# First six blocks of a gated linear attention as three pairs with two tokens per partition, in an order written out as a list

## Chip, cores and metric

One NeuronCore of a Trainium2 chip (trn2) runs the kernel; seven are idle. The metric is the device time of one execution in microseconds. The profile is of one execution, taken by the hardware profiler; its time and its span (first to last instruction) are both given below. Engines are named PE (TensorE; PEld its weight loads), DVE (VectorE), ACT (ScalarE), POOL (GpSimd) and SP (SyncE, which here only issues DMAs).

## Reference

```python
def _attn_ref(q, k, v, alpha):            # each (4, 8, 768, 48) float32
    state = np.zeros((B, H, D, D))
    for t in range(S):
        state = alpha[:, :, t, :, None] * state + np.einsum('bhd,bhe->bhde', k[:, :, t], v[:, :, t])
        y[:, :, t] = np.einsum('bhd,bhde->bhe', q[:, :, t], state)

def _moe_ref(x, w_in, w_out, s, b):       # x is y as (3072, 384); w_in (384, 2048), w_out (2048, 384)
    r = np.maximum(x @ w_in, 0.0)
    return (s * (r * r) + b) @ w_out
```

A gated linear attention (4 sequences, 8 heads of 48 channels, 768 steps) is followed by a two-layer block with a squared relu on its 3072 x 384 output.

## The kernel before, in words

The 3072 tokens are 24 blocks of 128; six blocks are one sequence. In a block a partition holds one token. Each block goes through a chain of small steps, whose functions are named `st_...`:

- `load` (L192) brings alpha, q, k and v as `a_in`, `q_in`, `k_in`, `v_in`: 128 x 8 rows of 48 floats, 192 bytes each, from SP's queue. `NIN` = 5 buffers of each.
- `st_ln` (L299, ACT) takes the logarithm of alpha into `la`; `st_cum` (L304, PE) sums it along the block by a product with an upper triangle, into `ct_ps`, and the last row by four products with a column of ones; `st_exp_b` and `st_exp_i` (L319, L322, ACT) make the decay `b_s`, its inverse `binv` and the block's total `blast`.
- `st_qb`, `st_kb` (L332, L337, DVE) scale q and k into `qk`; `st_vcast` (L326, POOL) casts v into `vp`.
- `st_T` with `st_Tcopy` (L345, L372: eight PE transposes and a DVE copy) turns `qk` into `qkT` for the first `NPE` = 8 blocks; for the others `st_Tdma` (L354) does it by a DMA transpose.
- `st_KV` (L360, PE), `st_t1` (L380, DVE) and `st_snew` (L396, POOL) carry the state `s_st` on.
- `st_A` (L402, PE) forms the scores in `a_ps`, `st_mask` (L414, DVE) masks them into `am`, `st_y` (L433, PE) forms the output transposed in `py_ps` from scores and old state, `st_yevac` (L466, ACT) copies it to `xd`. From block `NAY` = 9 on, `st_Ay` puts the scores of a block and the output of the one before it together.

Then the second part, by groups of blocks (`GROUPS`): `mm1` (L484) makes units of 512 columns (six products of 256 columns, or twelve of 128 in a group of one block) into one of two banks `h_ps`; `relu` (L498, ACT) and `square` (L501, DVE) follow, the result goes into a ring `gt` of 12 blocks; `mm2` (L510) makes a block's output in four quads of four products of 384 columns, in one of two banks `o_ps`; `oevac` (L523, DVE) scales it and adds the bias row; `ostore` (L535) stores it. The weights come in eight pieces of 768 KB through four staging buffers `wst`, are cast to bf16 by ACT (`cast_w_in` L247, `cast_w_out` L260), and the column sums of w_out for the bias are made by DVE (`colsum_part` L267, `colsum_add` L273) and a product (`bias_mm` L285).

What sets the order: every step is handed to `Schedule.op` (L51) with a duration, a priority (the block's due time plus an offset of the table `P`), and what it reads and writes. `Schedule.run` (L68) plays these through, and `emit` (L118) writes the instructions in the order of the starts so found; the first loads stand in the order of the list `LOADS` (L41). Where PE would idle ahead of the first `mm2`, `fill` (L683) puts in products of zeros of 256 columns (45 in all). On the chip each engine takes its instructions in that order.

## Time and profile before

| | |
|---|---|
| three runs | 194.94 us median (193.78 to 196.74) |
| the profiled execution | 193.93 us |
| its span, mean granted PE clock | 192.0 us, 0.991 |
| busy: PE, PEld, DVE, ACT, POOL | 175.3, 126.7, 135.9, 109.5, 33.3 us |
| DMA | 124,218 packets, 34.44 MB; 117,536 packets under 512 B |
| loads of a, q, k, v | 24 each, 192 KB, 3.7 to 3.9 us from issue to landing |
| weight loads | 8, 768 KB, 7.0 and 8.4 us |
| DMA transposes | 16, 3.7 us |

How to read it: times are microseconds from the span's start. A row of a group has the line, the engine, output and inputs, the shapes, the count, then busy time and the mean duration in ns, then the engine's idle time ahead of it and what ended that. Products are pipelined, so their durations overlap; the pace is read from the starts. The chain of waits follows the work that ended last back from the end, at each step to what released it. A DMA share of 1 means that the 16 DMA engines' packets together fill the time.

### The profile page before, as it was taken

What the parts mean: (1) busy time and instruction counts of PE and PEld (TensorE: products, weight loads), DVE (VectorE), ACT (ScalarE), POOL (GpSimd) and SP (SyncE); (2) the same over time, 40 slices, a digit from 0 to 9 for tenths busy, and PEclk for the clock granted to TensorE, in tenths of its full rate; (3) what the DMA queues carried; (4) which work ended last, traced back from release to release, by engine and by line L of the source; (5) the groups of instructions that cost most, each with busy time, mean ns of one, the idle gap of its engine ahead of it and who ended that gap; (6) DMA issues with size and microseconds to landing.
All of it is one profiled execution on the core that took longest, in us unless ns stands there. A gap on an engine that the chain in (4) does not pass through costs nothing.

```text
span 192.0 us, 5369 instructions
## 1 busy us (share of the span) xinstructions
PE 175.3 (91%) x2153; PEld 126.7 (66%) x2153; DVE 135.9 (71%) x256; ACT 109.5 (57%) x225; POOL 33.3 (17%) x60
## 2 busy tenths in 40 slices
PE   1877688879999999999999999999999999999992
PEld 0555467657677767777777766776766876777761
DVE  4643299989799898877689868587777786554421
ACT  3254789984357847767475754763663763654300
POOL 8402022103120431201122313011131131000000
PEclk9996999999999999999999999999999999999999
DMA  6989979999999999999999998897998895011112
GB/s 122 203 219 317 312 161 245 353 223 205 196 232 193 219 140 213 197 214 188 196 160 209 145 236 188 171 207 169 208 197 195 164 180 144 3 43 41 40 45 82
DMA packets 124218, 34.44 MB, mean 179 GB/s; under 512 B 117536, under 2 KB 122656, under 8 KB 124192
## 3 DMA queue, kind: packets, MB, share of 16 engines
q1 hardware_dynamic: 124192, 34.09, 82.6%
q8 instruction: 17, 0.28, 0.6%
q14 instruction: 9, 0.07, 0.1%
HBM read 25.17 MB, written 4.72 MB: 156 GB/s over the span
## 4 chain that ended last, share of the span: by engine, by line
PE 66%; DMA 14%; DVE 8%; SPq 7%; ACT 2%; issue 1%
PE o_ps L515 29%; PE h_ps L490 25%; PE py_ps L444 5%; DMA wst<-in_moe_w_in_dram 4%; DMA q_in<-in_q_dram 4%; SPq L194 4%; DMA wst<-in_moe_w_out_dram 3%; PE a_ps L406 3%; SPq L240 3%; DMA qkT<-qk 3%; DVE am L415 2%; PE py_ps L364 2%; PE ct_ps L306 1%; DVE gt L506 1%; ACT r L499 1%
## 5 line engine op out<-in xcount | busy, mean ns | idle before, releaser
L490 PE MATMUL h_ps<-xd,w_in_bf 128*128 128x256 bf16 (+1 forms) x624 | 74.8, 264 | 0.8 <-ACT r L499 0.5
L499 ACT ACTIVATE r<-h_ps 128x512 bf16<-128x512 f32 x96 | 56.5, 601 | 32.3 <-PE h_ps L490 22.8
L515 PE MATMUL o_ps<-w_out_bf,gt 128*128 128x384 bf16 x384 | 72.8, 326 | 2.0 <-ACT w_out_bf L261 2.0
L490 PEld LDWEIGHTS <-w_in_bf 128*128 128x128 bf16 x624 | 54.7, 98 | 10.8 <-issue 1.2
L506 DVE TENSOR_TENSOR gt<-r 128x512 bf16<-128x512 bf16 x96 | 43.5, 465 | 21.7 <-ACT r L499 21.1
L515 PEld LDWEIGHTS <-gt 128*128 128x128 bf16 x384 | 36.0, 98 | 21.2 <-issue 2.3
L415 DVE TENSOR_TENSOR am<-a_ps,mask 128x1024 bf16<-128x1024 f32 x24 | 29.3, 1220 | 1.6 <-PE a_ps L406 1.4
L327 POOL CAST vp<-v_in 128x384 bf16<-128x384 f32 x24 | 13.3, 553 | 95.0 <-DMA v_in<-in_v_dram 84.7
L526 DVE SCALAR_TENSOR_TENSOR o_sb<-o_ps,s_col,bias_w 128x384 f32<-128x384 f32 x24 | 14.8, 616 | 10.0 <-PE o_ps L515 9.6
L300 ACT ACTIVATE la<-a_in 128x384 bf16<-128x384 f32 x24 | 12.5, 521 | 14.1 <-DMA a_in<-in_alpha_dram 13.9
L400 POOL TENSOR_TENSOR s_st<-t,blast 128x384 bf16<-128x384 bf16 x16 | 14.5, 909 | 30.8 <-DVE t L389 23.0
L468 ACT ACTIVATE xd<-py_ps 128x384 bf16<-128x384 f32 x24 | 11.8, 491 | 13.0 <-PE py_ps L444 12.8
L338 DVE TENSOR_TENSOR qk<-k_in,binv 128x384 bf16<-128x384 f32 x24 | 13.4, 558 | 6.7 <-ACT binv L323 5.5
L333 DVE TENSOR_TENSOR qk<-q_in,b_s 128x384 bf16<-128x384 f32 x24 | 13.5, 564 | 5.2 <-ACT b_s L320 4.1
L320 ACT ACTIVATE b_s<-ct_ps 128x384 f32<-128x384 f32 x24 | 11.7, 488 | 6.8 <-PE ct_ps L311 6.7
L389 DVE TENSOR_TENSOR t<-py_ps,s_st 64x192 bf16<-64x192 f32 x32 | 11.3, 353 | 3.9 <-PE py_ps L364 3.2
L306 PE MATMUL ct_ps<-la,U_bf 128*128 128x384 bf16 x24 | 8.0, 334 | 6.3 <-ACT la L300 6.3
L323 ACT ACTIVATE binv<-ct_ps 128x384 f32<-128x384 f32 x24 | 11.8, 490 | 0.0
L311 PEld LDWEIGHTS <-la 128*128 128x128 bf16 x96 | 6.0, 97 | 7.7 <-issue 5.6
L406 PE MATMUL a_ps<-qkT 64*128 64x128 bf16 x192 | 9.8, 222 | 1.0 <-DVE qkT L373 0.7
L406 PEld LDWEIGHTS <-qkT 64*128 64x128 bf16 x192 | 5.5, 96 | 7.3 <-issue 4.3
L444 PE MATMUL py_ps<-am,vp 128*32 128x128 bf16 x384 | 9.8, 224 | 0.5 <-DVE am L415 0.5
(42 smaller groups left out, 108.1 us busy)
## 6 DMA issues: line engine op xcount, KB each, us to landing
a_in<-in_alpha_dram SPq DMA_DIRECT2D x24, 192.0 KB, 3.9
q_in<-in_q_dram SPq DMA_DIRECT2D x24, 192.0 KB, 3.9
k_in<-in_k_dram SPq DMA_DIRECT2D x24, 192.0 KB, 3.9
v_in<-in_v_dram SPq DMA_DIRECT2D x24, 192.0 KB, 3.7
out_dram<-o_sb SPq DMA_DIRECT2D x24, 192.0 KB, 2.6
wst<-in_moe_w_in_dram SPq DMA_DIRECT2D x4, 768.0 KB, 8.4
wst<-in_moe_w_out_dram SPq DMA_DIRECT2D x4, 768.0 KB, 7.0
qkT<-qk SPq DMA_TRANSPOSE x16, 3.7
```

Source lines behind the costliest of these rows:

```text
L327: nc.gpsimd.tensor_copy(out=vp_sb[n % 4].rearrange("a p (x d) -> a p x d", d=D)[:, :, 0:3:2, :], in_=v_in[n % NIN].rearrange("a (p e) d -> ...
L333: nc.vector.tensor_tensor(out=qk_sb[n % 3][:, 0, :, 0:D], in0=q_in[n % NIN], in1=b_sb[n % 2], op=ALU.mult)
L338: nc.vector.tensor_tensor(out=qk_sb[n % 3][:, 1, :, 0:D], in0=k_in[n % NIN], in1=binv_sb[n % 2], op=ALU.mult,)
L400: nc.gpsimd.tensor_tensor(out=s_sb[n % 3], in0=t1_sb[n % 2], in1=bl, op=ALU.mult)
L406: nc.tensor.matmul(out=a_ps[:, e, p, :], lhsT=qkT[64 * e : 64 * e + 64, 1, p, :], rhs=qkT[64 * e : 64 * e + 64, 0, p, :], start=True, stop ...
L415: nc.vector.tensor_tensor(out=am_sb[n % 2].rearrange("a e p t -> a (e p) t"), in0=a_ps.rearrange("a e p t -> a (e p) t"), in1=mask.unsquee ...
L444: nc.tensor.matmul(out=y_ps[32 * (x % 4) : 32 * (x % 4) + 32, x // 4, :], lhsT=(st[:, p, c0 : c0 + 32] if e is None else vp[:, p, c0 + 48 ...
L490: nc.tensor.matmul(out=hp[:, i * n : (i + 1) * n], lhsT=w_in_bf[:, kk, 128 * j : 128 * (j + 1)], rhs=xd_sb[g % 3][:, kk, 0:n], start=(kk = ...
L499: nc.scalar.activation(out=r_sb[w % 2], in_=h_ps[w % 2], func=AF.Relu)
L506: nc.vector.tensor_tensor(out=gt_sb[:, js[0] : js[0] + len(js), c0 : c0 + n], in0=r, in1=r, op=ALU.mult)
L515: nc.tensor.matmul(out=op[:, 0:d_model], lhsT=gt_sb[:, j, c0 : c0 + C], rhs=w_out_bf[:, j, :], start=(j == 0), stop=(j == NJ - 1),)
L526: nc.vector.scalar_tensor_tensor(out=ots, in0=o_ps[(x // 4) % 2][:, 0:d_model], scalar=s_col, in1=bias_w, op0=ALU.mult, op1=ALU.add,)
```

## The change

The first six blocks (one sequence) become three pairs. In a pair a partition holds two neighbouring tokens, so that a load brings rows of two tokens (384 bytes), and partitions 0 to 63 are the first block, 64 to 127 the second. Each step of the pair has its own function (`ld2`, `ln2`, `cum2`, `blk2`, `eb2`, `ei2`, `el2`, `vc2`, `mul2`, `T2`, `Tc2`, `KV2`, `A2`, `mk2`, `y2`); sums, scores and outputs are made for both tokens and both halves. The sums of pair 1 stand in the banks `h_ps`, those of the others in `ct_ps` and `py_ps`; scores use `a_ps` and `o_ps`. All 18 later blocks are transposed by DMA (`T1`), and scores and output go together from block 7 on (`Ay`). All groups of the second part have two blocks. There are three pair buffers of each input (`NIN` = 6), the ring holds 8 blocks, and two of the w_out pieces are staged in parts of the ring that are not yet in use.

The planner is gone: `PROGRAM` lists every step in order, with the engine for those that can run on several. Casts of weights, casts of v, relus, squares, column sums and some products with the decay now stand on ACT, DVE or POOL by name: of 96 squares 73 on DVE, 15 on ACT, 8 on POOL; of 96 relus 78 on ACT, 18 on DVE. Products of zeros (`F`, 120 columns) stand at three places, 33, 19 and 16 of them, behind the cumulative sums of pairs 0 and 1; none stands ahead of the first sum.

In the list a name is followed by its arguments: `ld2.a.0` loads alpha of pair 0, `ld_i.3` the fourth quarter of w_in, `ci`/`co` cast a quarter of w_in/w_out, `cp`/`ca` are the column sums, `mm1.g.u.w` is unit u of group g into bank w, `re.g.u.w.i` and `sq.g.u.i` are its relu from bank w into buffer i and its square from there, then the engine, `mm2.n.j` is quad j of block n, `ye`, `oe`, `st` evict y, evict and store the output of a block.

```diff
-GROUPS = [2, 1, 1, 2, 2, 2, 2, 2, 2, 2, 2, 2, 2]
+NPAIR = 3
+GROUPS = [2, 2, 2, 2, 2, 2, 2, 2, 2, 2, 2, 2]
+NIN = 6
-RING = 12
+RING = 8
 NST = 4
+STAGE = {0: 0, 1: 1, 2: 2, 3: 3, 6: 0, 7: 1}
+STAGE_GT = {4: 2, 5: 3}
+CUM_IN_H = [1]
-class Schedule:
...
+PROGRAM = """
+ld2.a.0 c_act c_U2 c_la.1 c_la.0 ld2.a.1 c_zeros ld2.v.0 c_half c_qk.0 ld2.q.0 c_t1.0 c_qk.1 c_mask2
+ld2.k.1 ld2.k.0 c_s.0 ld2.q.1 ln2.0 c_s.1 ld2.q.2 c_t1.1 ld_i.3 cum2.0.0 c_ident ld2.v.1 ln2.1 cum2.0.1
+c_U c_ones blk2.0 c_vp.1 eb2.0.1 cum2.1.0 c_s.2 ei2.0.0 cum2.1.1 c_vp.0 blk2.1 ei2.0.1 vc2.0.1.POOL
+el2.0 vc2.0.0.DVE eb2.1.0 mul2.q.0.1.DVE ei2.1.0 eb2.1.1 el2.1 mul2.k.1.0.DVE ei2.1.1 eb2.0.0
+mul2.k.1.1.DVE mul2.q.0.0.DVE mul2.k.0.0.DVE F.33 T2.0.0 mul2.k.0.1.DVE mul2.q.1.1.POOL KV2.0 ld1.k.7
+Tc2.0.0.ACT ld_i.1 T2.0.1 t1.0 mul2.q.1.0.POOL ld_i.2 ld2.a.2 t1.1 ld1.k.6 Tc2.0.1.DVE ld_i.0 ld2.k.2
+sn.1.DVE F.19 A2.0.0 ld_o.0 A2.0.1 ci.3.POOL mk2.0.0 ld1.a.6 ld2.v.2 mk2.0.1 F.16 T2.1.0 vc2.1.1.ACT
+vc2.1.0.POOL T2.1.1 Tc2.1.0.ACT Tc2.1.1.DVE y2.0 A2.1.0 ye.0.DVE ye.1.ACT A2.1.1 mk2.1.0 KV2.1 ci.1.ACT
+mm1.0.6.0 t1.2 mm1.0.7.1 re.0.6.0.0.ACT ld_o.3 mk2.1.1 sn.2.POOL ld1.a.7 re.0.7.1.1.ACT mm1.0.3.0 ld_o.1
+ci.2.ACT mm1.0.2.1 t1.3 sq.0.6.0.DVE sn.3.POOL y2.1 re.0.3.0.0.DVE sq.0.7.1.ACT ln2.2 re.0.2.1.1.DVE
+mm1.0.5.0 ye.2.DVE sq.0.3.0.ACT mm1.0.4.1 ye.3.ACT sq.0.2.1.DVE cum2.2.1 re.0.5.0.0.ACT ci.0.POOL
+cum2.2.0 blk2.2 re.0.4.1.1.ACT sq.0.5.0.DVE mm1.1.5.0 eb2.2.0 sq.0.4.1.DVE mm1.1.4.1 ei2.2.0
+re.1.5.0.0.DVE ld_o.2 eb2.2.1 mul2.k.2.0.POOL re.1.4.1.1.DVE mm1.0.0.0 el2.2 ei2.2.1 mul2.q.2.1.DVE
+mm1.1.0.1 sq.1.4.1.POOL sq.1.5.0.ACT co.0.DVE re.0.0.0.0.ACT mul2.k.2.1.POOL re.1.0.1.1.ACT mm1.1.2.0
+mul2.q.2.0.DVE ln1.6 sq.1.0.1.DVE mm1.1.1.1 cp.0.POOL re.1.2.0.1.DVE T2.2.1 vc2.2.1.ACT T2.2.0
+sq.1.2.1.DVE vc2.2.0.ACT mm1.1.3.0 re.1.1.1.1.DVE sq.0.0.0.POOL Tc2.2.1.ACT KV2.2 Tc2.2.0.DVE mm1.1.7.1
+sq.1.1.1.ACT co.3.POOL t1.4 re.1.3.0.0.ACT A2.2.0 A2.2.1 ln1.7 mk2.2.0 mm1.0.1.0 re.1.7.1.1.ACT ld1.a.13
+sn.4.POOL ld1.q.6 sq.1.7.1.ACT mm1.1.6.1 mk2.2.1 ld1.q.8 cp.3.POOL re.0.1.0.1.ACT ld_bs co.1.DVE y2.2
+cp.1.POOL sq.0.1.1.DVE ye.5.ACT ye.4.DVE mm2.0.0 co.2.ACT ld1.v.8 re.1.6.1.1.DVE cum1.6 ld1.a.10
+mm1.2.5.0 sq.1.3.0.POOL cp.2.DVE ld1.q.7 mm1.2.0.1 ld1.a.8 ei1.6 ca.2.3.DVE ld1.v.6 ca.0.1.POOL mm2.0.1
+eb1.6 ld1.k.8 sq.1.6.1.ACT cum1.7 re.2.5.0.0.DVE ld1.a.9 mm2.0.2 ei1.7 ld1.v.9 bm mm1.2.2.0 ld1.a.11
+re.2.0.1.1.DVE eb1.7 vc1.8.POOL ld1.v.7 mm2.0.3 sq.2.5.0.ACT ca.0.2.DVE sq.2.0.1.ACT mm1.2.3.1 ln1.10
+re.2.2.0.0.DVE bmm re.2.3.1.1.ACT mul1.q.7.DVE sq.2.2.0.ACT sq.2.3.1.DVE mm1.2.1.0 ln1.8 mul1.k.6.DVE
+cum1.8 bc re.2.1.0.0.ACT mm1.2.7.1 vc1.6.POOL mul1.q.6.DVE eb1.8 mm1.2.4.0 oe.0 T1.6 sq.2.1.0.ACT KV1.6
+mm2.1.0 re.2.7.1.1.ACT re.2.4.0.0.DVE ln1.9 mm2.2.0 t1.6 st.0 sq.2.7.1.ACT mm2.2.1 mul1.q.8.DVE
+vc1.9.POOL ei1.8 mm1.2.6.1 mul1.k.7.DVE sq.2.4.0.ACT mul1.k.8.DVE cum1.9 T1.7 ln1.11 mm2.1.1
...
+    def ld2(x, m):
+        b, c = 2 * m // NCH, 2 * m % NCH
+        nc.sync.dma_start(
+            out=whole(ins[x], m).rearrange("a s e -> a (s e)").rearrange("a (h f) -> a h f", h=H),
+            in_=src[x][b, :, c * C : (c + 2) * C, :].rearrange("h (p s) d -> p h (s d)", s=2),
+        )
...
+    def stage(i):
+        if i in STAGE_GT:
+            return gt_sb[STAGE_GT[i]].bitcast(FP32)[:, 0:QW]
+        return wst[STAGE[i]]
...
+    def ci(i, eng="ACT"):
+        copy_on(
+            eng,
+            w_in_bf[:, :, QW // 3 * i : QW // 3 * (i + 1)],
+            stage(i).rearrange("a (k f) -> a k f", k=3),
+        )
...
+    def b_ps(m, s):
+        return (h_ps if m in CUM_IN_H else (ct_ps, py_ps))[s]
...
+    def cum2(m, s):
+        l = whole(la, m)
+        for i in range(2):
+            nc.tensor.matmul(
+                out=b_ps(m, s)[:, 0 : H * D],
+                lhsT=U2x if i > s else U2,
+                rhs=l[:, i, :, 0:D],
+                start=(i == 0),
+                stop=(i == 1),
+            )
...
+    def blk2(m):
+        l = whole(la, m).rearrange("a s h d -> a s (h d)")
+        for p in range(NP):
+            for i in range(2):
+                nc.tensor.matmul(
+                    out=b_ps(m, 0)[:, 384 + 2 * p : 386 + 2 * p],
+                    lhsT=l[:, i, 128 * p : 128 * p + 128],
+                    rhs=half,
+                    start=(i == 0),
+                    stop=(i == 1),
+                )
...
+    def T2(m, x):
+        f = whole(qk, m)[:, :, x].rearrange("a s h d -> a s (h d)")
+        t_ps = a_ps[:, x, :].bitcast(BF16).rearrange("a (s p t) -> a s p t", s=2, p=NP)
+        for s in range(2):
+            for p in range(NP):
+                nc.tensor.transpose(
+                    out=t_ps[:, s, p, :], in_=f[:, s, 128 * p : 128 * p + 128], identity=ident
+                )
...
+    def KV2(m):
+        kb = whole(qk, m)[:, :, 1].rearrange("a s h d -> a s (h d)")
+        v4 = whole(vp, m).rearrange("a s p (x d) -> a s p x d", d=D)
+        cs = [c for c in range(2) if (2 * m + c) % NCH != NCH - 1]
+        for p in range(NP):
+            for s in range(2):
+                for c in cs:
+                    r = slice(64 * c, 64 * c + 64)
+                    nc.tensor.matmul(
+                        out=(py_ps, ct_ps)[c][:, 96 * p : 96 * p + 96],
+                        lhsT=kb[r, s, 128 * p : 128 * p + 128],
+                        rhs=v4[r, s, p, 0:3:2, :],
+                        start=(s == 0),
+                        stop=(s == 1),
+                    )
...
+    def A2(m, s):
+        T = whole(qkT, m)
+        dst = (a_ps, o_ps)[s]
+        for p in range(NP):
+            for e in range(2):
+                r = slice(64 * e, 64 * e + 64)
+                for c in range(2):
+                    t = slice(64 * c, 64 * c + 64)
+                    nc.tensor.matmul(
+                        out=dst[t, e, 128 * p : 128 * p + 128],
+                        lhsT=T[r, s, 1, p, t],
+                        rhs=T[r, :, 0, p, t],
+                        start=True,
+                        stop=True,
+                    )
...
+    def y2(m):
+        T, a2, v2 = whole(qkT, m), whole(am, m), whole(vp, m)
+        states = [c for c in range(2) if (2 * m + c) % NCH]
+        for i, (p, e, x) in enumerate(OWN):
+            c0 = 32 * x - 96 * p + 48 * e
+            for s in range(2):
+                for c in range(2):
+                    r = slice(64 * c, 64 * c + 64)
+                    nc.tensor.matmul(
+                        out=y_out((py_ps, ct_ps)[c], x),
+                        lhsT=v2[r, s, p, c0 : c0 + 32],
+                        rhs=a2[r, s, e, p, :],
+                        start=(i < 4 and s == 0),
+                        stop=(i >= 12 and s == 1 and c not in states),
+                    )
+        for c in states:
+            st = s_sb[(2 * m + c - 1) % 3]
+            for x in range(12):
+                p = x // 3
+                c0 = 32 * x - 96 * p
+                nc.tensor.matmul(
+                    out=y_out((py_ps, ct_ps)[c], x),
+                    lhsT=st[:, p, c0 : c0 + 32],
+                    rhs=T[:, :, 0, p, 64 * c : 64 * c + 64],
+                    start=False,
+                    stop=(x >= 8),
+                )
...
+    def re(g, u, w, i, eng="ACT"):
+        if eng == "ACT":
+            nc.scalar.activation(out=r_sb[i], in_=h_ps[w], func=AF.Relu)
+        else:
+            nc.vector.tensor_scalar(
+                out=r_sb[i], in0=h_ps[w], scalar1=0.0, scalar2=None, op0=ALU.max
+            )
...
+    def sq(g, u, i, eng="DVE"):
+        r = r_sb[i].rearrange("a (j t) -> a j t", j=4 // GROUPS[g])
+        if eng == "ACT":
+            nc.scalar.activation(out=unit_out(g, u), in_=r, func=AF.Square)
+        else:
+            on(eng).tensor_tensor(out=unit_out(g, u), in0=r, in1=r, op=ALU.mult)
...
+    def st(n):
+        dst = out[n * C : (n + 1) * C, :]
+        if n < NB2:
+            for s in range(2):
+                nc.sync.dma_start(
+                    out=dst.rearrange("(p s) m -> s p m", s=2)[s],
+                    in_=out_sb[n % 3][64 * s : 64 * s + 64],
+                )
+        else:
+            nc.sync.dma_start(out=dst, in_=out_sb[n % 3])
...
+    def F(n):
+        for _ in range(n):
+            nc.tensor.matmul(
+                out=h_ps[1][:, 392:512], lhsT=zeros[:, 0:128], rhs=zeros[:, 0:120], start=True, stop=True
+            )
...
+    ops = dict(locals())
+    for item in PROGRAM.split():
+        name, *args = item.split(".")
+        ops[name](*(int(x) if x.lstrip("-").isdigit() else x for x in args))
```

## Prediction

> **What bounds the kernel now.** I read the page's slices first, then the busy times by stretch, then the chain of waits in order of time, then the groups by shape for durations. The slices (40 of 4.8 us each):
>
> ```profile
> PE   1877688879999999999999999999999999999992
> ...
> DVE  4643299989799898877689868587777786554421
> ACT  3254789984357847767475754763663763654300
> ...
> DMA  6989979999999999999999998897998895011112
> ```
>
> From the tenth slice on PE is full, so that part can shrink only with PE's own work; what can be won lies in the first nine slices. There each of the others takes turns at being full:
>
> ```profile
> 15.00:20.00 5.00, 3.60 (x44) 2.50 (x44) 0.94 (x3) 1.49 (x1) 1.25 (x2) 0.66 1.03 326
> ...
> 25.00:30.00 5.00, 4.48 (x73) 3.54 (x72) 4.79 (x9) 4.77 (x10) 1.49 (x2) 1.00 0.88 227
> ...
> 35.00:40.00 5.00, 3.82 (x68) 2.81 (x66) 4.68 (x8) 4.90 (x9) 0.30 (x1) 1.00 1.10 349
> ```
>
> The columns are PE, PEld, DVE, ACT and POOL busy, the granted clock, the DMA share and GB/s. From 15 to 20 us nearly everything waits for DMA; from 25 to 40 DVE and ACT are full (4.8 of 5 us) while POOL idles. The chain says the same:
>
> ```profile
> 13.87 8.26 DMA wst<-in_moe_w_in_dram
> 22.15 1.49 ACT w_in_bf L248
> ...
> 25.47 6.15 DMA wst<-in_moe_w_out_dram
> ...
> 34.60 8.07 DMA q_in<-in_q_dram
> 42.69 0.56 DVE qk L333
> ...
> 47.14 0.57 PE py_ps L444 x28
> 47.73 2.11 PE o_ps L515 x12
> ...
> 180.67 7.81 PE o_ps L515 x48
> 188.51 0.62 DVE o_sb L526
> ```
>
> DMA, ACT and DVE alternate until 47.1 us; from there it is PE almost alone to 188.5. So "PE dense from" is the number to forecast. The tail (last eviction and store) is 192.0 - 188.5 = 3.5 us, and the execution took 193.93 us, 1.93 more than its span and 1.0 under the median of 194.94.
>
> **PE's work.** The chain's pieces give PE's pace: 0.65 us for four L515 products (a quad) and for six L490 products (a unit), 0.33 for L406, 0.51 for 28 of L444 (0.34 for 16), 0.45 for eight transposes; the PE timeline adds 0.27 for a cumulative sum and 0.17 for L364. Counted behind 47.14 us, the old kernel has 80 units, 92 quads, 19 L406, 20 L444 sets, 19 L364, 18 sums, 3 transposes: 52.2 + 59.8 + 6.3 + 9.7 + 3.2 + 4.9 + 1.4 = 137.5 us, in 141.3 us of time. 3.8 us are seams, such as the 0.1 us ahead of each L406.
>
> **The change, part by part.**
>
> *Loads.* Twelve pair loads replace 24: the same bytes, half the packets, 384 B each. Old rows: ACT's wait for the first `a_in` ends at 3.71 us and that for the seventh load at 9.34, so 0.94 us each (195 to 219 GB/s in one-us stretches); stretches full of weights run at 360 to 404 GB/s, so 2.1 us per 786 KB. A pair load lies between 0.94 (only packets count) and 1.88 (only bytes count); on 16 engines 0.94 us is 64 packets of 15 ns, and 2.1 us is 24 packets of 2 KB at 87 ns; the straight line between gives 22 ns for 384 B, 1.4 us a load, which I take. In the new order the first `a` lands at about 4.2, the first weights (`ld_i.3`) at 16, `ld_i.1` and `ld_i.2` at 20.5 and 22.6, `ld_i.0` at 27, `ld_o.0` 30.5, `ld_o.3` 35, the last (`ld_o.2`) 40 to 41: where the old ones end too (the last cast waits until 41.06), but with six blocks' inputs in, not four. Bounds of 0.94 and 1.88 move the last weight by -6 and +6 us. SP's own share is hidden: an issue is 0.4 to 0.8 us, and an issue already stretched to 4.49 us while data flowed.
>
> [...]
>
> *Attention of the pairs.* Per pair PE gets four 384-column sums for two, 16 transposes as before, 16 L437 products for 8, 32 score products for 16, and 64 + 24 (pair 0: 64 + 12) of y for 56. By the rows' time per product (18 ns in L444, 41 in L406, 43 in L364) a pair is 0.9 + 0.9 + 0.7 + 1.3 + 1.6 = 5.4 us, against 3.5 for two old blocks. If 64x64 tiles overlap better, scores fall to 0.6; that is the low end, -1.0 per pair. Nearly all of this falls before PE is dense, so it costs there only through the chain.
>
> *First chain.* `ln2.0` (0.84 by the line through 521 ns for 384 and 1483 for 1536) ends at 5.0; sums and last rows 6.6; then ACT has eight exponentials and two small ones, 0.38 pitch: 10.4. The 33 products of zeros wait for `ei2.1.1` (10.1); at 0.055 us (120 columns at full clock) or 0.10 (half clock, as the first zeros of the old trace show, 0.24 for 256) they end at 11.9 or 13.4, and the transposes stand behind them on PE. Then T, L437, T: 13.5 to 15; on DVE t1 twice (1.5), copy 0.69, state 0.4; scores 1.3, two masks 2.4, y 1.4; DVE's `ye.0` starts at about 21.6, and with pair 1's scores ahead of it on PE the first unit at 23.2, against 21.04 in the old trace. So this stage gets about 2 us longer, not shorter, but brings four blocks nearly through, not three.
>
> *To dense.* From `ye.0` to `re.2.0` DVE has four masks of 1.22, three t1 of 0.71, copies of 0.69 and 3 x 0.55, eight relus at 0.67 (bounds 0.56 and 0.75: the 558 ns copy of 384 from PSUM, as it is and by size), seven squares at 0.42, two products 1.1, two w_out casts at 1.0 (bounds 1.0 and 2.2: the 0.69 copy of 1024 and the 0.56 one of 384, by size; I take the one nearer in size), column sums 1.9, `bm` 0.3: 23.0 us. On the old timeline an instruction starts 0.08 ahead of the end of the one before it, which takes off 1.8; at the 95% that DVE reaches between 25 and 40 us, the 21.2 left take 22.3: 43.9. ACT has about 19 us in the same time (its squares at 0.60, the row of L499 at the same size). POOL has, from about 30 us, three column sums 1.8, three squares 1.2, a cast of 1536 1.8 (bounds 1.7 and 2.0, with and without a fixed part), a state update and a product 0.9: 12.6 us, by these rows and their sizes:
>
> ```profile
> L327 POOL CAST vp<-v_in 128x384 bf16<-128x384 f32 x24 | 13.3, 553 | 95.0 <-DMA v_in<-in_v_dram 84.7
> ...
> L400 POOL TENSOR_TENSOR s_st<-t,blast 128x384 bf16<-128x384 bf16 x16 | 14.5, 909 | 30.8 <-DVE t L389 23.0
> ```
>
> That ends `sq.1.3.0` at 43 to 45; `re.2.5`, the next user of that buffer, waits for it, with `bm`, `re.2.0` and `ca.0.2` queued behind it on DVE and `mm1.2.2` on PE. So I take the later end, 45.0.
>
> [...]
>
> *Behind it.* Left when PE becomes dense: 78 units 50.9, 94 quads 61.1, 16 sums 4.3, 15 sets of line 565 2.6, 18 scores 5.9, 18 y 8.7, bias 1.4: 134.9, with the old 3.8 of seams 138.7. ACT's next 11 us of work start two us earlier than PE's 9, so I add nothing; without that lead it costs 1.8. The two added DMA transposes (1.2 to 2.2 us of SP each) pass on a queue whose stretches now show gaps (shares of 0.41 to 0.7); if loads ran late, the cost is again a PE wait, bounded by the one in the old trace (0.25 us at 111.4).
>
> *Sum.* 45.0 + 138.7 + 3.5 = 187.2 of span, + 1.93 = 189.1 for such an execution, 4.8 under the old one; the old median lay 1.0 above its profiled execution, the new one should lie about as much: **190.0 us**, 2.5% under 194.94. About 2% is what a measurement of this kernel can tell: below 191.0 is faster, above 198.8 slower.
>
> **Rivals.**
> 1. *Nothing gained* (191 to 196): DVE and ACT are already full from 25 to 40 us, the pairs' products are added work, and an order written out cannot move when a load is late. If DVE works at its old 85% (19.58 of 23 us between 21 and 44) dense is at 46.5, and with the ACT lead lost the end is 1.5 + 1.8 later, 193.3. Against it: casts, relus and squares now move between three engines.
> 2. *POOL becomes the bound, slower*: `vp` casts last 502 ns at best and 952 at worst, while DVE is at work: 1.9 times. If all of POOL's 12.6 us stretch so, `sq.1.3.0` ends at 30 + 23.9 = 53.9, dense is 8.9 later, the end at 198.9. It decides from that factor, or from a smaller one if POOL starts its part late (at 1.6, from 34 us on). For it: DVE is never idle then. Against it: the median cast is 507 ns.
> 3. *PE dense from its first unit*: behind 23.2 us PE has 96 units 62.7, 96 quads 62.4, pair 2 and `y2.1` 7.0, single blocks 22.1, bias 1.4: 155.6, + 3.8 + 3.5 + 1.93 + 1.0 = 189.0, only one less than the forecast. With scores at 0.6 and no delay by the zeros the first unit comes at 21 and 0.7 less is left: 186.
>
> **How the numbers follow.** Forecast, 187.5 to 191.0: 0.39. Rival 3 below that: 0.10. Rival 1: 0.33. Rival 2 and beyond: 0.18. Faster 0.49, same 0.33, slower 0.18. The range, 185.5 to 198, runs from half a us below rival 3 to nearly where POOL decides; the forecast's own is 187.5 to 191.0.
>
> **What would show it.** Right: pair loads landing 1.4 us apart; the first unit (line 668) at 23; DVE over 90% from 22 to 45; PE without waits behind 45; 138 us from there to the end. Wrong: POOL casts and squares well over 1.2 us with DVE or PE waiting for POOL; PE waits for the last weights; a granted clock under 0.9 between 10 and 25 us; waits for `qkT` by DMA after 60 us.

## The result and the profile after

The changed kernel takes 205.72 us (median of four runs, 205.48 to 206.68) where the old one took 194.36 on the same chip (193.54 to 196.74): a ratio of 1.061, with a 95% interval of 1.054 to 1.068. It is slower by 11.4 us; 190.0 had been forecast, with 198 as the upper end. The profiled execution has a span of 204.9 us at a mean granted clock of 0.992. Chips differ by up to a per cent (the old kernel's medians are 192.6 to 194.4 us), so the experiments below are compared by their ratio to the old kernel on the same chip; 0.01 of it is 1.9 us. A ratio leaves out runs that are over 1.5% above the fastest run of their kernel.

The slices (40 of 5.1 us) of the changed kernel:

```profile
PE   0687898386899999699999999989898999998872
...
DVE  2349789889988698866789667588488698444121
ACT  4821798165694226338557465764583664653000
POOL 8534158859133136320015010310022210000000
...
DMA  6999999836997989789899999797993522010211
```

PE reaches 9 in the sixth slice (26 to 31 us) and then falls back to 3 in the eighth (36 to 41 us); it is full from the twelfth on, not the tenth, and later slices show a 6 and some 8s where the old kernel had only nines. DVE and POOL are high together in slices 7, 8 and 10. DMA drops to 3 in the ninth. By stretches (columns as before):

```profile
25.00:30.00 5.00, 4.85 (x118) 3.77 (x117) 4.85 (x9) 4.60 (x7) 3.29 (x3) 1.00 1.04 336
30.00:35.00 5.00, 4.42 (x44) 3.53 (x43) 4.61 (x7) 4.43 (x11) 3.47 (x3) 1.00 1.04 294
35.00:40.00 5.00, 2.82 (x34) 1.99 (x32) 4.83 (x4) 1.73 (x3) 5.00 (x4) 1.00 1.05 341
40.00:45.00 5.00, 3.30 (x45) 2.28 (x45) 3.58 (x7) 2.75 (x5) 2.14 (x3) 0.66 0.13 29
45.00:50.00 5.00, 3.23 (x103) 2.05 (x102) 5.00 (x6) 2.46 (x3) 5.00 (x4) 1.00 0.78 148
```

Read the counts, not only the busy times. From 35 to 40 us DVE is busy for 4.83 us with four instructions; from 25 to 30 it did nine in the same time. PE has 2.82 and ACT 1.73 us of work there: both wait for DVE, while POOL is full. After that pause PE gets 0.66 of its clock. The chain of waits in that stretch, and at the end:

```profile
32.94 1.72 DVE w_out_bf L306
34.66 1.27 DVE qk L406
35.93 1.96 DVE gt L697
...
38.74 1.73 DVE gt L697
...
46.14 2.08 DVE w_out_bf L306
48.23 1.18 DVE gt L697
...
189.71 2.77 PE o_ps L702 x16
192.49 0.02 issue
192.51 0.63 DVE o_sb L711
193.14 0.04 issue
193.18 1.47 PE o_ps L702 x8
```

In the first stretch it is DVE almost alone, with squares of 128x512 that take 1.2 to 2.0 us where they had taken 0.42. At the end the old chain had 48 products in one piece of 7.81 us; now each lot of quads stops for an eviction. PE's waits say the same in sum (us in total, times, longest):

```profile
PE o_ps L702 <- DVE o_sb L711: 5.8, 7, 1.7
...
PE h_ps L668 <- DVE r L680: 5.1, 4, 2.1
```

An account of where PE loses time, estimated from counts and the pace of each kind of product. Products of zeros count as lost, and most of what the prediction called seams (3.8 us) counts as work here. The pace of the small products is known only roughly, so an entry can be off by one or two microseconds:

| us lost by PE | to the first unit | from there to 54 us (old: 47) | behind it | tail |
|---|---|---|---|---|
| old kernel | 17.5 | 5.4 | 0.6 | 3.5 |
| changed | 17.2 | 10.6 | 9.7 | 4.0 |

PE's work, the span less the losses, is about the same (165.0 and 163.4 us). The start is neither better nor worse; 5 us are lost before PE is full, and 9 behind it.

### The profile page after: what moved, and what is told of

Read it like the earlier page. It is cut to its first block, busy times and chain, and to the rows that moved or that the text cites. A ratio compares the mean times of both kernels' runs of the same rounds, so it can differ in the third digit from the quotient of the medians.

```text
span 204.9 us, 5511 instructions
## 1 busy us (share of the span) xinstructions
PE 175.4 (86%) x2266; PEld 126.8 (62%) x2266; DVE 143.8 (70%) x247; ACT 105.5 (51%) x211; POOL 58.4 (28%) x84
## 3 DMA queue, kind: packets, MB, share of 16 engines
q1 hardware_dynamic: 113920, 34.61, 76.1%
## 4 chain that ended last, share of the span: by engine, by line
PE 56%; DVE 19%; DMA 13%; ACT 4%; SPq 3%; issue 3%; DVEq 0%; ACTq 0%
PE o_ps L702 23%; PE h_ps L668 18%; DMA qkT<-qk 9%; DMA a_in<-in_alpha_dram 4%; SPq L262 3%; PE py_ps L600 3%; DVE gt L697 3%; DVE o_sb L711 3%; PE a_ps L578 2%; DVE am L462 2%; DVE r L680 2%; DVE w_out_bf L306 2%; DVE qk L548 2%; PE h_ps L733 2%; DVE t L636 1%
## 5 line engine op out<-in xcount | busy, mean ns | idle before, releaser
L668 PE MATMUL h_ps<-xd,w_in_bf 128*128 128x256 bf16 x576 | 73.5, 275 | 5.7 <-DVE r L680 5.1
L678 ACT ACTIVATE r<-h_ps 128x512 bf16<-128x512 f32 x78 | 46.3, 596 | 26.2 <-PE h_ps L668 21.0
L697 DVE TENSOR_TENSOR gt<-r 128x512 bf16<-128x512 bf16 x73 | 36.7, 512 | 18.1 <-ACT r L678 17.6
L711 DVE SCALAR_TENSOR_TENSOR o_sb<-o_ps,s_col,bias_w 128x384 f32<-128x384 f32 x24 | 14.8, 616 | 15.7 <-PE o_ps L702 15.5
L587 DVE TENSOR_TENSOR am<-a_ps,U 128x1024 bf16<-128x1024 f32 x18 | 22.0, 1220 | 1.4 <-PE a_ps L578 1.2
L548 DVE TENSOR_TENSOR qk<-q_in,b_s 128x384 bf16<-128x384 f32 x18 | 12.6, 703 | 2.0 <-DMA q_in<-in_q_dram 1.0
L695 ACT ACTIVATE gt<-r 128x512 bf16<-128x512 bf16 x15 | 9.5, 634 | 8.3 <-DVE r L680 8.2
L511 ACT ACTIVATE la<-a_in 128x384 bf16<-128x384 f32 x18 | 9.4, 522 | 7.8 <-DMA a_in<-in_alpha_dram 7.5
L680 DVE TENSOR_SCALAR r<-h_ps 128x512 bf16<-128x512 f32 x18 | 12.2, 684 | 1.4 <-DVE gt L697 0.5
L304 ACT ACTIVATE xd<-py_ps 128x384 bf16<-128x384 f32 x18 | 8.8, 490 | 7.1 <-PE py_ps L600 7.0
L697 POOL TENSOR_TENSOR gt<-r 128x512 bf16<-128x512 bf16 x8 | 10.0, 1260 | 5.9 <-DVE r L680 5.9
L536 ACT ACTIVATE binv<-ct_ps 128x384 f32<-128x384 f32 x18 | 8.7, 485 | 1.7 <-PE ct_ps L524 1.7
```

The source lines that it names most:

```text
L548: on(eng).tensor_tensor(out=half_of(qk, n)[:, "qk".index(x), :, 0:D], in0=half_of(ins[x], n).rearrange("a (h d) -> a h d", d=D), in1=half_ ...
L587: nc.vector.tensor_tensor(out=half_of(am, n).rearrange("a e p t -> a (e p) t"), in0=a_ps.rearrange("a e (p t) -> a (e p) t", t=128), in1=U ...
L668: nc.tensor.matmul(out=h_ps[w][:, i * n : (i + 1) * n], lhsT=w_in_bf[:, kk, 128 * j : 128 * (j + 1)], rhs=xd_sb[g % 3][:, kk, 0:n], start= ...
L678: nc.scalar.activation(out=r_sb[i], in_=h_ps[w], func=AF.Relu)
L680: nc.vector.tensor_scalar(out=r_sb[i], in0=h_ps[w], scalar1=0.0, scalar2=None, op0=ALU.max)
L697: on(eng).tensor_tensor(out=unit_out(g, u), in0=r, in1=r, op=ALU.mult)
```

## Where DVE's time goes: two timelines side by side

DVE's instructions of the stretch (start, duration), and below POOL's:

```profile
32.87 1.79 DVE L306 CAST w_out_bf<-gt 128x1536 bf16<-128x1536 f32 x1
34.58 1.35 DVE L406 TENSOR_TENSOR qk<-q_in,b_s 128x384 bf16<-128x384 f32 x1
35.86 2.03 DVE L697 TENSOR_TENSOR gt<-r 128x512 bf16<-128x512 bf16 x1
38.02 0.69 DVE L680 TENSOR_SCALAR r<-h_ps 128x512 bf16<-128x512 f32 x1
38.74 1.72 DVE L697 TENSOR_TENSOR gt<-r 128x512 bf16<-128x512 bf16 x1
...
44.93 1.21 DVE L462 TENSOR_TENSOR am<-o_ps,mask 128x1024 bf16<-128x1024 f32 x1
46.06 2.17 DVE L306 CAST w_out_bf<-gt 128x1536 bf16<-128x1536 f32 x1
48.15 1.25 DVE L697 TENSOR_TENSOR gt<-r 128x512 bf16<-128x512 bf16 x1
```

```profile
32.49 1.35 POOL L697 TENSOR_TENSOR gt<-r 128x512 bf16<-128x512 bf16 x1
33.81 1.71 POOL L406 TENSOR_TENSOR qk<-k_in,binv 128x384 bf16<-128x384 f32 x1
35.48 2.12 POOL L322 TENSOR_TENSOR colsum<-gt 128x768 f32<-128x768 f32 x1
37.56 1.22 POOL L697 TENSOR_TENSOR gt<-r 128x512 bf16<-128x512 bf16 x1
38.73 1.46 POOL L306 CAST w_out_bf<-wst 128x1536 bf16<-128x1536 f32 x1
...
45.59 1.82 POOL L322 TENSOR_TENSOR colsum<-gt 128x768 f32<-128x768 f32 x1
47.36 1.76 POOL L697 TENSOR_TENSOR gt<-r 128x512 bf16<-128x512 bf16 x1
```

Add start and duration, and set each end on DVE against the end of the POOL instruction that was under way when it started. The square at 35.86 ends at 37.89; POOL's sum had ended at 37.60, 0.29 earlier. The one at 38.74 ends at 40.46, POOL's cast at 40.19 (0.27). The one at 48.15: 49.40 and 49.12 (0.28). The casts: 34.66 and 33.84 (0.82), 48.23 and 47.41 (0.82). So these DVE instructions, squares, casts, products and sums that take their large inputs from SBUF, stand until POOL's has ended, and end behind it by a time that is fixed for their kind; they are not slowed in proportion. The relu at 38.02 and the mask at 44.93, whose large input lies in PSUM, take their usual 0.69 and 1.21 beside a busy POOL. POOL waits the other way round: its square from 47.36 takes 1.76 and not 1.22, since DVE's cast held on until 48.23. Summed over the eight DVE instructions of the list (the times alone are 0.95 for a cast, 0.55, 0.42 and 0.94), the waits are 0.84 + 0.80 + 1.61 + 1.30 + 1.22 + 0.83, and 0.56 and 0.34 for two column sums behind 50 us: 7.5 us.

So each engine stood for the other: DVE for 7.5 us in all, POOL's square for about 0.5, and the two instructions that read PSUM not at all (0.69 and 1.21 us). The prediction had no price for it.

The old trace held the same sign. Ten of its 96 squares take 0.62 to 1.05 us instead of about 0.42, and each of the ten ends 0.27 or 0.28 us behind an instruction of POOL; together that is 3.7 us. One of them, and POOL beside it:

```profile
69.40 1.05 DVE L506 TENSOR_TENSOR gt<-r 128x512 bf16<-128x512 bf16 x1
```

```profile
69.06 1.10 POOL L400 TENSOR_TENSOR s_st<-t,blast 128x384 bf16<-128x384 bf16 x1 [1.25 <-ACT blast L324]
```

The mean of that row (465 ns) hid them.

## Experiments

The changed kernel itself was not run again on the chips of the experiments. Four of its variants below that gained little or nothing have ratios of 1.058 to 1.067 there, so its 1.061 serves as the reference.

**One cause at a time.** Four edits of the changed kernel, on one chip.

Loads of blocks 6 to 9 earlier:

```diff
-... mul2.q.2.0.DVE ln1.6 ... ln1.7 mk2.2.0 mm1.0.1.0 re.1.7.1.1.ACT ld1.a.13 sn.4.POOL ld1.q.6 ... ld1.q.8 ... ld_bs ...
+... mul2.q.2.0.DVE ld1.q.6 ld1.q.7 ld1.v.6 ld1.v.7 ld1.a.8 ld1.q.8 ld1.v.8 ld1.k.8 ld1.a.9 ld1.v.9 ld_bs ln1.6 ...
+... ld1.a.11 ld1.a.13 ...
```

> Only the order of SP's loads changes: those of blocks 6 to 9 (and b, s) stand right behind the last weight load, and alpha of block 13, which waits for the logarithm of block 7, stands behind alpha of block 11. Queue theory (the head of SP's queue holds up the loads, 33.5 to 43.3 us without an issue): if the 9.7 us that PE loses behind 45 us come mostly from late loads, the time falls by 4 us or more, to 202 or less. Lock theory (DVE's list from 30 to 54 us is stretched by POOL, whatever the loads do): PE is dense at 54 as now, the time falls by 0 to 1.5 us (205 to 204), only the PE waits for qkT and for the logarithm of later blocks may shrink. A rise of a microsecond is possible if the earlier loads take DMA time from the last two weight loads.

Ratio 1.067 (1.058 to 1.075): nothing gained. The issues of the changed kernel had this hole, and it closed (the next issue now comes at 33.31):

```profile
33.45 0.71 SPq L291 DMA_DIRECT2D wst<-in_moe_w_out_dram  x1
43.25 0.37 SPq L262 DMA_DIRECT2D a_in<-in_alpha_dram  x1
```

But DVE's list ran as before (squares of 2.02, 1.72 and 1.25 us). A hole of nine us in the issues, with the DMA idle for some four us of it (a share of 0.04 from 40 to 44), is conspicuous and was not on the path.

The output bank as two tiles:

```diff
-    o_ps = ps.tile([128, 2, 512], FP32, name="o_ps")
+    o_ps = [ps.tile([128, 512], FP32, name=f"o_ps{i}") for i in range(2)]
...
-                out=o_ps[:, n % 2, 0:d_model],
+                out=o_ps[n % 2][:, 0:d_model],
```

> The output bank is two tiles instead of one tile of two halves; the second mask of a pair becomes two instructions of half the size. Whole-tile theory (a product into one half waits for the eviction of the other half): the seven PE waits of 5.8 us for DVE's o_sb go, of which four of 0.71 us stand in the last 16 us and one each at 157 and 85; the time falls by 4 to 5.5 us, to about 200.5 to 201.5. Rival (these waits are real reuse of the same half, or PE is held up next by something else): under 2 us.

Ratio 1.045 (1.039 to 1.052), 3.0 us less. With one tile, products into one half had waited for the eviction of the other half; in the same order of quads, the waits for `o_sb` fall from 5.8 us to 0.2, and the end is one piece again:

```profile
PE o_ps L711 <- DVE o_sb L720: 0.2, 1, 0.2
```

```profile
184.15 11.21 PE L711 MATMUL o_ps<-w_out_bf,gt 128*128 128x384 bf16 x68
```

Of the 5.8 us of waits 3.0 came back, less than expected; in this profile DVE's list ran about 2.5 us later (its first cast of w_out at 35.55 instead of 32.87), and whether the other runs did the same is not known.

Column sums on PE:

```diff
-... cp.0.POOL ... cp.3.POOL ... cp.1.POOL ... cp.2.DVE ... ca.2.3.DVE ... ca.0.1.POOL ... ca.0.2.DVE ...
...
-        for e in range(2):
-            nc.tensor.matmul(out=o_ps[:, 1, 0:d_model], lhsT=bones, rhs=colsum[0][...], ...)
+        for j in range(NJ):
+            nc.tensor.matmul(out=o_ps[:, 1, 0:d_model], lhsT=bones, rhs=w_out_bf[:, j, :], ...)
```

> The column sums of w_out are made by 16 PE products on the bf16 weights (so the bias uses rounded weights) instead of four additions of halves and three of partial sums on POOL and DVE; 7.7 us of POOL work and 3.7 us of DVE time (as now measured) go from the stretch 35 to 55 us, PE gets 16 products of 0.16 us for two of 0.35, 1.9 us more. Lock theory (a DVE instruction that works from SBUF to SBUF starts only when the POOL instruction under way ends): the square at 35.9 us lasts 0.4 to 0.5 instead of 2.03, the cast at 46.1 about 0.85 instead of 2.17; DVE's list ends 5 to 7 us sooner, the time falls by 3 to 5 us. Speed theory (DVE is slow there for another reason, the clock or SBUF writes by DMA): the squares stay over 1.2 us, the time falls by 0 to 1.5.

Ratio 1.040 (1.035 to 1.045), 4.0 us less, as the lock theory said. The square that had met POOL's sum now meets POOL's square, and where POOL idles both instructions have their own durations:

```profile
35.65 1.26 DVE L696 TENSOR_TENSOR gt<-r 128x512 bf16<-128x512 bf16 x1
...
43.26 0.95 DVE L305 CAST w_out_bf<-gt 128x1536 bf16<-128x1536 f32 x1
44.13 0.42 DVE L696 TENSOR_TENSOR gt<-r 128x512 bf16<-128x512 bf16 x1
```

PE is full from 45 us, the time that the prediction had named. The waits for `o_sb` grew to 7.4 us, eight of them where there had been seven: a PE that is earlier met more of the evictions. The edit also takes 3.7 us of work off DVE, so by itself it does not separate the lock from a DVE that has too much to do; splitting POOL's instructions (below) does. The two fp32 products that it replaces had taken 1.29 us together, not twice 0.35, so PE's added work is 1.3 us and not 1.9.

Squares and relus exchanged between DVE and ACT:

```diff
-re.1.0.1.1.ACT ... sq.1.0.1.DVE ... sq.1.2.1.DVE ... re.0.1.0.1.ACT ... sq.0.1.1.DVE
+re.1.0.1.1.DVE ... sq.1.0.1.ACT ... sq.1.2.1.ACT ... re.0.1.0.1.DVE ... sq.0.1.1.ACT
```

> Three squares (128x512, SBUF to SBUF) go from DVE to ACT, and two of the relus ahead of them (PSUM to SBUF) from ACT to DVE, all between 35 and 50 us; no work is taken away, POOL is as before. Lock theory: a relu from PSUM takes 0.69 us beside POOL, a square from SBUF 0.42 plus the rest of POOL's instruction; DVE saves the 2.03, 1.72 and 1.25 us and gains twice 0.69, ACT gets 3 x 0.60 - 2 x 0.6: PE is dense 2 to 3.5 us sooner, the time is 202 to 204. Load theory (DVE has simply too much to do, nothing waits): saving 3 x 0.42 and adding 2 x 0.69 changes nothing, the time stays within 0.7 us of 205.7, or rises if ACT becomes the later one.

Ratio 1.058 (1.051 to 1.064), 0.6 us less, inside the intervals: a miss for the size that the lock theory named. The relus on DVE took 0.68 and 0.69, as it says, but the waits moved on to the next instructions that work in SBUF: the cast takes 2.43 instead of 2.17 and the column sum 2.49 instead of 1.50, each ending 0.81 or 0.82 behind POOL's. With POOL's work still there, something else on DVE met it. In this profile the first cast of w_out also started 1.7 us later than in the changed kernel (34.61 and 32.87), so what the exchange alone is worth is not separated.

**The lock itself, and the zeros.**

```diff
-        add_on(eng, colsum[i], w[:, 0 : QW // 2], w[:, QW // 2 : QW])
+        n = 4 if eng == "POOL" else 1
+        z = QW // 2 // n
+        for x in range(0, QW // 2, z):
+            add_on(eng, colsum[i][:, x : x + z], w[:, x : x + z], w[:, QW // 2 + x : QW // 2 + x + z])
```

> The four POOL additions for the column sums are cut into four pieces of 192 columns each; the work is the same, on the same engines, in the same places. Lock theory (a DVE instruction from SBUF to SBUF waits until the POOL instruction under way has ended, then runs at its own speed, and POOL's next one waits for it): a wait is now at most one piece, 0.5 to 0.6 us, so the square at 35.9 us takes 0.4 to 1.0 instead of 2.03, the cast at 46.1 0.9 to 1.5 instead of 2.17; POOL itself gets longer by its own waits. Time: 0.5 to 2.5 us less. [...]

Ratio 1.045 (1.035 to 1.054), 3.1 us less with the same work on the same engines; the interval just touches that of the changed kernel, and the gain is above the 0.5 to 2.5 us expected. In the profile DVE's list ends at 50.2 us instead of 54.0. This is what a lock held for the length of an instruction does. A slowing in proportion to the overlap, which four pieces leave about as it was, would have left the square at 2.03 and the cast at 2.17 us; they take 0.81 and 1.34:

```profile
35.64 0.81 DVE L703 TENSOR_TENSOR gt<-r 128x512 bf16<-128x512 bf16 x1
...
42.49 1.34 DVE L306 CAST w_out_bf<-gt 128x1536 bf16<-128x1536 f32 x1
```

POOL pays: its first sum takes 2.92 us in four pieces for 2.12 in one.

```diff
-F.33
+F.8
```

> The first lot of zero products (ahead of the first transposes) has 8 products instead of 33; the other two lots stay. Zeros theory (33 products at 0.105 us each end at 13.3 us, 2 us behind DVE's product of q and b that the transposes need): the first transposes start near 11.3 us, the first unit 1 to 2 us sooner, and if that goes through to the end the time falls by 1 to 2 us. Stage theory (the stretch 30 to 54 us is set by DVE's list and by weights that land when they land): the first unit comes sooner, but PE is dense at 53 to 54 as before; the time falls by less than 0.8 us. Clock rival: the transposes and the first products behind it run at half the clock, and the first unit is not sooner at all.

Ratio 1.058 (1.050 to 1.067). The transposes start at 11.00 instead of 13.30 and the first unit at 21.87 instead of 23.53, and the end does not move beyond the intervals.

```diff
-cum2.0.0
+F.30 cum2.0.0
```

> One edit on the changed kernel: 30 more products of zeros ahead of the first cumulative sum, where the old kernel had some. Clock theory (the 33 products behind the sum run at half the clock, 0.105 us each, because PE did nothing before): they now take 0.055 each and end near 11.9 instead of 13.3 us, the eight transposes 0.6 instead of 0.95; the first unit comes 1 to 1.8 us sooner, the time falls by 0.5 to 1.5 us. Stage theory (from 30 us on DVE, not PE's start, sets the time): the first unit is sooner, the time within 0.8 us of the changed kernel's, a ratio of 1.057 to 1.063 to the kernel before. Side question: in the runs so far PE stops for 0.6 to 2.7 us at its 450th instruction (the 52nd product of the first output, or, with 50 instructions less, the first score of pair 1) with nothing to wait for in the trace; 60 instructions more should move that stop into the transposes of pair 1 or the products of zeros ahead of them.

Ratio 1.059 (1.051 to 1.067). With PE at work before them, the 33 products come 0.053 us apart instead of 0.100, as the clock theory has it, although the granted clock of the profile is 1.00 there in both kernels. The transposes behind them start at 10.81 and take 0.61, the first unit comes at 20.29, 3.2 us sooner, and nothing arrives at the end: by the account above PE loses 1.4 us less up to 25 us and 1.2 us more from 30 to 45. The place of the zeros, a part of the change, costs nothing that can be measured here. The side question was answered otherwise than expected: no stop appeared.

**Together.** First the edits of "the output bank as two tiles" and "column sums on PE" in one kernel, with no other change.

> Two tiles for the output bank and the column sums on PE together (the bias uses bf16-rounded weights). If the two causes are separate, their gains add: 3.0 + 4.0 us alone, and the waits for o_sb that were 7.4 us with the sums on PE go: 205.7 less 7 to 10 us, 196 to 199 on a chip where the kernel before takes 194.4, a ratio of 1.01 to 1.02. If they share one critical stretch, the gain is that of the larger one plus at most 1 us, a ratio of 1.035 or more.

Ratio 1.023 (1.011 to 1.034): 7.5 us less than the changed kernel, about the sum of 3.0 and 4.0. The gains add, as those of two separate causes do.

Then that kernel with the loads earlier and fewer zeros:

```diff
-F.33 ... ld1.a.13 ... ld1.q.6 ... ld_bs ...
+F.8 ... mul2.q.2.0.DVE ld1.q.6 ... ld1.v.9 ld_bs ... ld1.a.11 ld1.a.13
```

> As the one before, with the loads of blocks 6 to 9 behind the last weight and 8 zero products instead of 33 in the first lot (bias from bf16-rounded weights). With DVE no longer late, the first unit and the loads may now count: 1 to 3 us under the one before, a ratio of 0.995 to 1.01 to the kernel before. If neither counts, within 0.7 us of it. If this is not below 1.0, the pairs themselves bring nothing on this kernel: what is left over the old one is then PE's added work of 1.9 us for the sums and a later first unit.

Ratio 1.048 (1.040 to 1.056), 5 us worse than without. The edit itself has a fault: `ld_bs` now stood behind ten loads, and DVE waited 3.71 us for `b_col`, until 52.6, with the relus of two units behind it. That this wait is most of the 5 us is likely and was not isolated; whether the earlier loads or fewer zeros would gain anything without it, this run does not tell.

Then two tiles and sums on PE again, with less on POOL:

```diff
-sq.1.4.1.POOL ... sq.0.0.0.POOL ... sq.1.3.0.POOL ... mul2.k.2.0.POOL ... mul2.k.2.1.POOL
+sq.1.4.1.ACT ... sq.0.0.0.ACT ... sq.1.3.0.ACT ... mul2.k.2.0.DVE ... mul2.k.2.1.DVE
```

> Two output tiles and the sums on PE (bias from bf16-rounded weights) as before; in addition the three squares that POOL has before 50 us go to ACT and its two products of k of pair 2 to DVE, so that POOL has only one cast there. Lock theory: DVE's cast at 35 us falls from 1.80 to 0.9, the product at 36.7 from 1.36 to 0.55, the squares at 38 and 40 from 1.25 and 0.74 to 0.42; DVE gains 2.9 and gets 1.1 us more work; PE is dense 1 to 2 us sooner, the time falls by 1 to 2 us below the kernel with the two edits alone, a ratio of 1.012 to 1.018. If ACT becomes the later one instead, no gain or a loss of up to 1 us.

Ratio 1.015 (1.007 to 1.022), as named, though the 1.5 us below the kernel with the two edits alone are inside the intervals. DVE's first cast takes 0.95, one square still meets POOL's last cast (1.65). PE's account for this kernel: 17.4 us lost to 25 us, 4.2 from there to 50, 5.5 behind it.

**What is left behind 50 us.** All but the old kernel's variant have the edits of the kernel above. First, every load of blocks 12 to 23 moves right behind the last reader of its buffer, and `ld_bs` behind `ld_o.2`.

> As the one before, with every load of blocks 12 to 23 put into SP's queue right behind the last reader of its buffer (110 steps of the list earlier on average) and the loads of b and s behind the last weight. Queue theory: the PE waits for qkT, for the logarithm and for v behind 80 us (0.3 to 0.6 us each, 3 to 4 us in all with what follows them) go, the time falls by 2 to 3 us below the one before. Rival: these waits are not from late loads but from the transposes and from DVE and ACT being busy then; the time is within 0.8 us, or rises because early loads take DMA time from the ones that are due.

Ratio 1.093 (1.086 to 1.101), 15 us worse. SP issued its entries in the order of the list (from 61.5 us on three loads, then the transpose at 63.95), and the DMA transposes now stood behind loads: PE's waits for `qkT` rose from 2.3 us in the kernel above to 9.0, one of them 4.87.

A warm start:

```diff
-cum2.0.0
+F.30 cum2.0.0
```

> Two output tiles, sums on PE (bias from bf16-rounded weights), no squares on POOL, and 30 zero products ahead of the first sum, which alone brought the first unit 3 us forward and nothing at the end. If DVE and POOL were what hid it, it now counts: 1 to 2.5 us less than without, a ratio of 1.002 to 1.010. If the weights' landing or the late waits set the end, it is within 0.8 us of it, 1.011 to 1.019.

Ratio 1.021 (1.014 to 1.028): no gain, if anything a loss of 1.3 us. With the start earlier, ACT waits for alpha (2.06 us at 52.1) and DVE for q (1.84 at 49.3).

With that start, each load of blocks 12 to 23 up to 25 steps earlier:

> As the one before, with the loads of blocks 12 to 23 up to 25 steps of the list earlier (110 on average cost 15 us: the DMA transposes then stood behind loads). Queue theory: PE's waits for v, for alpha and the q load behind 80 us go, 1 to 2 us less than the one before. Transpose theory: the waits for qkT stay or grow, the time is the same or up to 3 us more.

No ratio: one run took 197.9 us, the other three 203.2 to 204.3, so nothing is concluded but that it is not faster (c5_warm took 195.8 to 197.3).

With the warm start, both kinds of output stores from ACT's queue:

```diff
-            nc.sync.dma_start(out=dst, in_=out_sb[n % 3])
+            nc.scalar.dma_start(out=dst, in_=out_sb[n % 3])
```

> As c5_warm, with the stores of the outputs issued from ACT's queue instead of SP's, so that no load and no transpose stands behind a store that waits for the eviction of an output. Queue theory: SP waits 4 to 5 us less between 60 and 150 us, the waits for qkT, alpha and v shrink, 1 to 2.5 us less than c5_warm. Rival: ACT, which takes its instructions in order, waits for DVE's evictions in SP's place and delays relus: the same time or up to 3 us more.

Ratio 1.020 (1.010 to 1.029), the same as c5_warm. Taking the stores off SP's queue brings nothing; whether ACT lost what SP gained was not separated.

The old kernel with one output tile:

```diff
-    o_ps = [ps.tile([128, 512], FP32, name=f"o_ps{i}") for i in range(2)]
+    o_both = ps.tile([128, 2, 512], FP32, name="o_ps")
+    o_ps = [o_both[:, i, :] for i in range(2)]
```

> The old kernel with its two output banks as two halves of one tile, nothing else changed. Whole-tile theory: each product into one half waits for the eviction of the other, as in the changed kernel, where that cost 3 us; PE shows waits for o_sb of 0.5 to 0.7 us, up to one a block, the time rises by 2 to 6 us, a ratio of 1.01 to 1.03. If the waits in the changed kernel came from the order of its quads alone (two blocks interleaved), the old kernel, which does one block after the other more often, rises by less than 1 us.

Ratio 1.034 (1.023 to 1.046). The old kernel, with nothing else changed, gets the waits that it did not have:

```profile
PE o_ps L516 <- DVE o_sb L527: 4.1, 8, 0.7
```

So the single tile costs the old kernel time too, in its own order of quads. The waits are 4.1 of the 6.6 us by which it is slower.

The warm start with the loads of blocks 6 to 11 in the order of use:

```diff
+mul2.q.2.0.DVE ld_bs ld1.a.10 ld1.v.8 ld1.q.7 ld1.q.6 ld1.a.8 ld1.v.6 ld1.q.8 ld1.a.9 ld1.k.8 ld1.v.9 ld1.a.11 ld1.v.7
+ln1.7 ld1.a.13
```

> As c5_warm (two output tiles, sums on PE with bias from bf16-rounded weights, no squares on POOL, 30 zero products ahead of the first sum), with the loads of blocks 6 to 11 and of b and s right behind the last weight load, in the order of their use. Queue theory: no idle DMA at 38 to 41 us, no wait for alpha or q at 48 to 53; PE is dense from 45, 1.5 to 3 us less than c5_warm, a ratio of 1.005 to 1.013. Rival: the waits only move to the next late load; within 0.8 us of it, 1.017 to 1.025.

Ratio 1.020 (1.011 to 1.029): no gain.

The same without `F.30`:

> As c8_loads_due, without the 30 zero products ahead of the first sum. If the warm start counts once the loads are in time, this one is 1 to 2 us over c8_loads_due; if not, they are within 0.8 us of each other, and both 1 to 2.5 us under the kernel without POOL squares (1.0145), if the queue theory holds.

Ratio 1.006 (1.001 to 1.012), the lowest of all, but it rests on four of ten runs, and the ten lie between 192.21 and 196.69 us. The medians of all runs on that chip are 195.42 for this kernel, 197.17 for the one with the warm start and 192.6 for the old one; 195.42 to 192.6 is 1.015, the ratio of c3_no_pool_squares. So it is not shown that the order of the loads brings anything, and why a warm start should cost is open. No version tried is faster than the old kernel.

## Why the prediction was wrong, point by point

- *Loads*: right. ACT waits for the first two pair loads until 4.24 and 5.42 us, DVE for the next two until 7.04 and 8.37: 1.38 us a load for the 1.4 that was taken between 0.94 and 1.88. The 1.88 did not come.
- *First chain*: right. The first unit starts at 23.53, forecast 23.2; the zeros end at 13.3, the later of the two bounds. That an earlier first unit brings nothing to this kernel was shown by e4 and e8.
- *Attention of the pairs*, 5.4 us of PE each: too dear. Sixteen score products take 0.25 us (16 ns each, not 41), 64 of y about 0.8; a pair comes to some 3.9 us, the low end and below. It did not matter, since PE waits in that stretch.
- *To dense*: **the step that failed first.** "At the 95% that DVE reaches between 25 and 40 us, the 21.2 left take 22.3: 43.9" priced each DVE instruction by its row in the old trace, and POOL's 12.6 us beside it. In the old trace POOL had mostly idled beside these rows, and the wait of one engine for the other was put at nothing. The list took 31.6 us (22.4 to 54.0), 9.3 more than the 22.3 forecast, and 7.5 of it are waits for POOL, so PE was dense at 54 and not at 45.0. Splitting POOL's instructions gave 3.1 us of the time back, taking the sums away 4.0.
- *Behind it*: **the step that failed second.** "3.8 of seams" and a PE wait "bounded by the one in the old trace (0.25 us)" left out what the diff shows in its declarations and the description of the change does not mention: `o_ps`, two tiles before, is one tile of two halves. PE waited 5.8 us for evictions, and two tiles gave 3.0 us back. The rest, 9.7 - 5.8 = 3.9 us, is mostly waits that go back to DMA transposes and loads (PE waits 1.3 us for `qkT`, 0.8 each for a logarithm and for a product with the decay; another 1.2 for relus on DVE). They were in the list of what would show the prediction wrong, with no price, and no edit took them away.
- *Rival 2* had the place (POOL beside DVE) and 198.9 us, and the direction wrong: it let POOL stretch because DVE works, and it is DVE, with 95% of its time taken, that stands. The range ended at 198, below rival 2's own 198.9, and no case had two causes.
- *POOL's squares*: 1.04 to 1.35 us on POOL, leaving out the one of 1.76, against 0.42 on DVE, 2.5 to 3.2 times, so the 1.2 in the sum was about right. What counted was POOL's hold on DVE (7.5 us of waits), not POOL's own pace.
- *How much of the miss is shown.* The time lies 15.7 us above the forecast. The two repairs together gave 7.5 us back, about half of it. The other half is not shown by an edit. By the account for c3_no_pool_squares it stands behind 50 us, where PE still loses 5.5 us against 0.6 in the old kernel; up to there the losses are about the old ones (21.6 and 22.9 us), where the forecast had counted on a gain.

What stays open: why the kernel with both repairs is still 1 to 2% behind the old one instead of ahead of it, although six blocks' inputs come in half the packets. PE's losses up to the first unit are those of the old kernel (17.2 and 17.5 us), so the pairs' start gains nothing; the waits behind 50 us were not removed by any order of the loads that was tried.

## What to carry to other kernels

Before moving work from DVE to POOL, mark each DVE instruction of that stretch that works from SBUF to SBUF: here its price was its own time plus most of what was left of the instruction that POOL had under way (a square of 0.42 us took 2.03). Keep POOL's instructions there short, or take them out: here the one gave 3.1 us back, the other 4.0. Look at the slowest of a row, not only at its mean (1.05 us and 465 ns for the old squares). Compare tile declarations in a diff as closely as instructions: give two halves that are reused in turn two tiles, as one tile cost the changed kernel 3.0 us and the old one 6.6. Find the engine that sets a stretch before working on an earlier start or an idle DMA: here three earlier starts of 1.7 to 3.2 us arrived as nothing.

## What the hardware showed besides

In nine of the kernels PE stopped for 0.8 to 2.3 us in the middle of the first output of a pair, with no wait in the trace, while the DMA was full (a share of 0.96 over the first 25 us in the kernel with both repairs). The wait of the kernel with both repairs:

```profile
PE ct_ps L496 <- issue: 2.3, 1, 2.3
```

Thirteen products of that output follow the stop in each of them, so it stands at the 52nd of 64, and that is the 450th instruction of PE in the profile's records, weight loads counted. In the two kernels with 50 instructions less ahead of it (25 products of zeros, each with its weight load), the 450th is the first score of pair 1. In one of them PE stands there for 2.41 us, for which the profile names another releaser; in the other for 0.69, no longer than the changed kernel does at this score without any stop. So the place seems to go with the count of instructions, not with the code, by that one run. What PE stands for there was not shown; the page of the changed kernel lists a queue of the kind `instruction` with 17 packets and 0.28 MB, and no trace ties the stop to it. The stop is absent from the changed kernel's own profiled execution, where PE came there later (21.19 us), and from the kernels with a warm start.
